# Splits of the second transform's matrices ahead of the data's own splits, and two output stores on another queue

## The chip, the cores and the metric

The kernel runs on one core of a Trainium2 chip. The metric is device time in microseconds (us) of one execution. An engine works through its own instructions in the order in which they were written, and waits only where a semaphore tells it to: TensorE (PE in the profile; PEld is its weight load), VectorE (DVE), ScalarE (ACT), GpSimd (POOL) and SyncE (SP). DMA transfers are issued by SP, ACT or POOL, each from its own queue in order.

## The reference, cut to what matters

The inputs are x (2048 x 640), two 2048 x 2048 matrices cr and ci, two 640 x 640 matrices wr and wi, and the two weights and biases of an MLP with 1536 hidden units, all in float32.

```python
xn = layernorm(x)
a = einsum("sd,ed->se", xn, wr); b = einsum("sd,ed->se", xn, wi)
y = einsum("ts,se->te", cr, a) - einsum("ts,se->te", ci, b)
out = x + y + gelu(xn @ w1 + b1) @ w2 + b2
```

## The kernel before, in words

Every product of two float32 matrices is made of three matmuls (`product`, L302 to L307): each operand is split into a high part in a reduced float32 format and a low part, the rest, and high times high, high times low and low times high are summed (L305, L306, L307). Low times low is left out. A split is a copy to the reduced format (`high`, on ACT, L191) followed by a subtraction (`low`, on DVE, L194). So before a matmul can run, somebody has split both of its operands.

The sequence transform is made first: xn stands still as weights (tiles `xab` and `xc`), and the columns of cr and ci move through the array. Its results, u from cr and v from ci, stay as sums in tiles `u1`, `u2`, `u` and `v1`, `v2`, `v`. The second transform then multiplies these sums by wr and wi. Both use a scheme that replaces eight products of blocks by seven, so each stage runs through seven products w = 0 to 6, and every product works on sums and differences of blocks, which are called forms here.

This case is about the second transform, the stage "y". It is run twice, each time for a pair of time tiles of 512 rows: a first pair (about 596 to 668 us in the profile) and the last pair (about 766 us to the end). In it the forms of wr and wi stand still as weights, five chunks of 128 columns for each product, and the sums u and v move. A product is done in steps u: step 0 uses chunks 0 and 1, step 1 the next two, step 2 the fifth. In the last pair step 3 adds two chunks of the MLP's second weight, whose hidden units were kept for this. "w4u1" below is step 1 of product 4. With three matmuls for each block, products 0, 1 and 2 have 18, 18 and 9 matmuls in steps 0 to 2 and products 3 to 5 have 12, 12 and 6; the last pair's step 3 has 18 or 12. Product 6 has 45 matmuls in the first pair. In the last pair it has 42 matmuls of 512 columns, and then 42 of 256 columns.

Three streams feed a step, and each has its own engines and buffers:

- The weights' forms. `load_g` (L1653, its DMA is L1672, on SP's queue) brings raw form number i = 5w + position into one of 7 places (first pair: `ws` x3, `gr_a` x2, `gr_b` x2) or 13 places (last pair: also six in `xab`). The load into a place is issued when the step that used it is written, and so it waits for that step's matmuls. `split_g(b, stop)` (L1677) then splits all forms below `stop`: the high part on ACT (L191), the low part on POOL (L1682), not on DVE.
- The moving forms. `form(n)` (L551) splits the sums for step n: high on ACT, low on DVE, into one of 3 slots of `as` (five slots in the last pair, two of them in `r`). The slot is free when the matmuls of the step before in it are through, so the form that is written in step n waits for step n's matmuls (first pair: it is for step n + 3; last pair: n + 5). ACT stands in that wait.
- The work beside (`hidden_beside`, L1685): additions on DVE that make the next sums, copies out of the matmuls' accumulators (`copy`, L1720, on ACT), transposes, and output stores (`store`, L1358).

At the end of each step the loop at L1941 writes: the work to be done ahead (`pre`), then the moving forms that are due, then the work beside (`post`), then `split_g`. That is the order on ACT. The stores of the last pair's outputs go to queues that are named in the call: `out_a` (L1731) for tile 1's columns, `out_b` (L1757) for tile 2's.

Of the kernel before, what the change touches and what calls it, by code (L numbers as in the profile page):

```python
# [17 lines left out]
B = 32  # L18
# [9 lines left out]
def kernel(  # L28
# [45 lines left out]
    nc = tc.nc  # L74
# [8 lines left out]
    ND = D // P  # L83
# [106 lines left out]
    def high(h, s):  # L190
        nc.scalar.activation(h, s, AF.Copy)  # L191
# [11 lines left out]
    def rows_of(ap, t):  # L203
        return ap[t * TB : (t + 1) * TB].rearrange("(n r) d -> r n d", r=B)
# [329 lines left out]
    def steps_in(st):  # L534
        return 2 if st[0] == "s" else ND // 2 + 1 if st is not stages[-1] else NLATE
# [164 lines left out]
    last = 1  # L700
# [653 lines left out]
    def store(t, src, c0, c1, *queues):  # L1354

        queues = queues or (nc.sync,)
        for q in range(Q):
            queues[q % len(queues)].dma_start(  # L1358
                rows_of(out, t)[:, :, q * DQ + c0 : q * DQ + c1], src[q * B : (q + 1) * B]
            )  # L1360
# [316 lines left out]
    def split_g(b, stop):  # L1677

        for i in range(split_to.get(b, 0), min(stop, NW * ND)):
            h, l = (GT[b, i][:, k] for k in range(2))  # L1680
            high(h, l.bitcast(F32))
            nc.gpsimd.tensor_tensor(l, l.bitcast(F32), h.bitcast(F32), op=ALU.subtract)  # L1682
        split_to[b] = max(stop, split_to.get(b, 0))

    def hidden_beside(b, n):  # L1685


        ta, tb = blocks[b - 1][1], blocks[b][1]
        last = b == len(blocks) - 1
        x_, y_, z_ = (banks[:, k : k + 2] for k in (X, Y, Z))  # L1690
        us, vs = bank(US), bank(VS)
        ya = yo[ta]

        def s(which, k):
            return sums[(ta, tb)[which], k]
# [14 lines left out]
        def columns(k):  # L1710

            return s(1 if last else 0, ("u1", "u2")[k]).rearrange("p a b -> p (a b)").rearrange("p (n e) -> p n e", n=NB)
# [16 lines left out]
            return f  # L1729

        def out_a(c0, c1):  # L1731
            return lambda: store(ta, ya[:, :, c0:c1], c0, c1, nc.gpsimd if c0 else nc.sync) if last else None

        def first_two():
            add(A["two"][:, 2:], A["two"][:, 2:], y_)
            to(ya[:, :, : 2 * B], A["two"][:, 2:], f"ya2_{ta}", out_a(0, 2 * B))()
# [18 lines left out]
            return f  # L1755

        def out_b(k):  # L1757
            return lambda: store(tb, columns(k), 2 * k * B, 2 * (k + 1) * B, *(((nc.gpsimd,), (nc.sync, nc.scalar))[k] if last else ()))

        def last_columns():  # L1760

# [166 lines left out]
    for kind, what in stages:  # L1928
        b = blocks.index(what) if kind == "s" else b
        count = NW * steps_in((kind, what)) if (kind, what) != stages[-1] else NW * NLATE  # L1930
        for n in range(first, first + count):
            w, u = entries[n][2:]
            if kind == "s":
                sequence_entry(n, what, w, u)
                pre, post = beside(*what, n - first)
            else:
                hidden_entry(n, b, w, u)
                pre, post = hidden_beside(b, n - first)
            for f in later:
                f()  # L1940
            later.clear()  # L1941
            for f in pre:
                f()
            while made <= n + 3 + min(max(n - LASTY + 2, 0), 2):
                form(made)
                made += 1
            for f in post:
                f()
            if kind == "y":
                done = w * ND + (min(2 * u + 2, ND) if u < 3 else ND)  # L1950
                split_g(b, done + (4 if u < 3 else ND))
        first += count
        if n + 1 < len(entries):
            X, Y, Z = Y, Z, X
        if kind == "y":
            put_off.clear()
# [45 lines left out]
```

## Time and profile before

| | us |
|---|---|
| median of the timed executions | 876.92 (lowest 876.74) |
| profiled execution | 871.97 |
| its span | 870.2 |
| PE busy | 848.1 (97%) |
| DVE busy | 703.8 (81%) |
| ACT busy | 387.6 (45%) |
| POOL busy | 162.8 (19%) |

In rows of the timeline the first number is the start in us from the span's start, the second the duration in us; then come engine, line, operation and tiles, and in brackets the idle time of that engine just before, with what ended it. A matmul's duration covers its way through the array, and the next one starts before it is over, so the pace of PE is read from start to start. In rows of the windows, each stretch has its length and then for PE, PEld, DVE, ACT and POOL the busy time and in brackets the number of instructions, followed by the granted clock, the DMA share and GB/s. Some matmul records can be missing.

### The profile page before, as it was taken

The page shows a single profiled execution, that of the slowest core. Times are in us where ns is not written, and L with a number is a line of the kernel's source. Part 1 is how long each engine was busy: PE and PEld are TensorE (multiplying, and loading weights), DVE is VectorE, ACT ScalarE, POOL GpSimd, SP SyncE. Part 2 cuts the span into 40 slices and gives each one's busy share as a digit, 9 for nine tenths or more (in the row PEclk, how much of TensorE's full clock was granted, in tenths as well). Part 3 has the DMA queues.
Part 4 walks back from the last instruction along what each step waited for, and adds up shares of the span by engine and source line. Part 5 has one row for each costly group of instructions (what it writes and reads, how often), then busy time and mean ns, then how long its engine had stood idle before and what let it go on. Part 6 is the DMA issues. An engine that isn't in the chain of part 4 may idle for free.

```text
span 870.2 us, 10835 instructions
## 1 busy us (share of the span) xinstructions
PE 848.1 (97%) x3719; PEld 695.6 (80%) x3719; DVE 703.8 (81%) x865; ACT 387.6 (45%) x566; POOL 162.8 (19%) x211
## 2 busy tenths in 40 slices
PE   8999999999999999999999999999989999999887
PEld 7888888888888888888888888887867888878665
DVE  6979886558478898898878799896988888768993
ACT  7655654444466634443433423233453232555450
POOL 3340021145000000000000000012753000334453
PEclk9999999999999999999999999999999999999999
DMA  7996576699689794965365985372226992261333
GB/s 228 283 253 167 125 193 203 188 282 294 222 241 419 180 207 114 230 156 159 85 182 162 293 198 134 96 186 63 79 77 182 268 268 72 82 254 43 86 87 73
DMA packets 197255, 154.69 MB, mean 178 GB/s; under 512 B 58000, under 2 KB 177808, under 8 KB 196688
## 3 DMA queue, kind: packets, MB, share of 16 engines
q1 hardware_dynamic: 185984, 122.73, 54.5%
q0 software_dynamic: 9040, 30.74, 10.5%
q10 hardware_dynamic: 2176, 0.52, 0.3%
q8 instruction: 29, 0.48, 0.2%
q14 instruction: 26, 0.21, 0.1%
HBM read 108.08 MB, written 41.94 MB: 172 GB/s over the span
## 4 chain that ended last, share of the span: by engine, by line
PE 83%; issue 6%; POOL 5%; DVE 3%; DMA 2%; SPq 1%; ACT 0%; POOLq 0%; DVEq 0%; ACTq 0%
PE banks L307 25%; PE banks L305 24%; PE banks L306 24%; PE banks L327 9%; POOL gr_b L1682 1%; POOL xab L1682 1%; POOL gr_a L1682 1%; POOL ws L1682 1%; DVE as L194 1%; SPq L1672 0%; DMA row<-in_A_x_dram 0%; DMA u<-ys 0%; DMA xab<-wsum 0%; DVE xab L453 0%; DMA ws<-wsum 0%
## 5 line engine op out<-in xcount | busy, mean ns | idle before, releaser
L191 ACT ACTIVATE as<-r 128x1024 fp32r<-128x1024 f32 x80 | 85.0, 1062 | 172.0 <-PE banks L307 148.0
L306 PE MATMUL banks<-as,xab 128*128 128x512 f32 (+1 forms) x375 | 145.5, 388 | 0.0
L307 PE MATMUL banks<-as,xab 128*128 128x512 f32 (+1 forms) x375 | 145.5, 388 | 0.0
L305 PE MATMUL banks<-as,xab 128*128 128x512 f32 (+1 forms) x375 | 145.4, 388 | 0.0
L194 DVE TENSOR_TENSOR as<-r,as 128x1024 fp32r<-128x1024 f32 x80 | 97.2, 1216 | 38.7 <-ACT as L191 38.6
L305 PE MATMUL banks<-as,xc 128*128 128x512 f32 x244 | 94.9, 389 | 0.0
L306 PE MATMUL banks<-as,xc 128*128 128x512 f32 x244 | 94.9, 389 | 0.0
L307 PE MATMUL banks<-as,xc 128*128 128x512 f32 x244 | 94.9, 389 | 0.0
L1682 POOL TENSOR_TENSOR ws<-ws 128x384 fp32r<-128x384 f32 (+1 forms) x24 | 31.6, 1328 | 321.4 <-DVE u L453 297.3
L306 PEld LDWEIGHTS banks<-as,xab 128*128 128x128 f32 x375 | 70.4, 188 | 14.5
L305 PEld LDWEIGHTS banks<-as,xab 128*128 128x128 f32 x375 | 70.4, 188 | 14.4
L307 PEld LDWEIGHTS banks<-as,xab 128*128 128x128 f32 x375 | 70.4, 188 | 14.4
L191 ACT ACTIVATE as<-rt 128x1024 fp32r<-128x1024 f32 x37 | 39.3, 1062 | 76.9 <-PE banks L307 61.2
L327 PE MATMUL banks<-xt,xab 128*128 128x512 f32 x240 | 56.6, 390 | 0.0
L194 DVE TENSOR_TENSOR as<-rt,as 128x1024 fp32r<-128x1024 f32 x37 | 45.5, 1230 | 12.2 <-ACT as L191 12.1
L306 PEld LDWEIGHTS banks<-as,xc 128*128 128x128 f32 x244 | 45.8, 188 | 9.5
L305 PEld LDWEIGHTS banks<-as,xc 128*128 128x128 f32 x244 | 45.8, 188 | 9.5
L307 PEld LDWEIGHTS banks<-as,xc 128*128 128x128 f32 x244 | 45.8, 188 | 9.5
L327 PEld LDWEIGHTS banks<-xt,xab 128*128 128x128 f32 x240 | 45.0, 188 | 9.3
L305 PE MATMUL banks<-hs,xc 128*128 128x512 f32 x120 | 46.7, 389 | 0.0
L306 PE MATMUL banks<-hs,xc 128*128 128x512 f32 x120 | 46.7, 389 | 0.0
L307 PE MATMUL banks<-hs,xc 128*128 128x512 f32 x120 | 46.7, 389 | 0.0
(316 smaller groups left out, 1790.7 us busy)
## 6 DMA issues: line engine op xcount, KB each, us to landing
raw<-in_A_dft_seq_re_dram SPq DMA_DIRECT2D x64, 256.0 KB, 5.3
raw<-in_A_dft_seq_im_dram SPq DMA_DIRECT2D x64, 256.0 KB, 5.0
w1r<-in_B_w_dram SPq DMA_DIRECT2D x144, 80.0 KB, 3.2
forms_ab<-xab SPq DMA_DIRECT2D x4, 1280.0 KB, 9.6
row<-xn SPq DMA_DIRECT2D x14, 320.0 KB, 6.0
w2r<-in_B_w_dram SPq DMA_DIRECT2D x12, 320.0 KB, 4.9
forms_c<-xc SPq DMA_DIRECT2D x4, 896.0 KB, 7.7
wturn<-row POOLq DMA_DIRECT2D x10, 320.0 KB, 4.2
```

What stands on the lines that cost most here:

```text
L191: nc.scalar.activation(h, s, AF.Copy)
L194: nc.vector.tensor_tensor(l, s, h.bitcast(F32), op=ALU.subtract)
L305: nc.tensor.matmul(acc, wh, mh, start=first, stop=False, skip_group_check=goes_on)
L306: nc.tensor.matmul(acc, wh, ml, start=False, stop=False, skip_group_check=goes_on)
L307: nc.tensor.matmul(acc, wl, mh, start=False, stop=last, skip_group_check=goes_on)
L327: nc.tensor.matmul(acc, W1[i][:, a, j * P : (j + 1) * P], XT[j][:, b], start=n == 0, stop=n == len(steps) - 1)
L1682: nc.gpsimd.tensor_tensor(l, l.bitcast(F32), h.bitcast(F32), op=ALU.subtract)
```

## The change

Two things change, in this stage alone.

First, `split_g` is called ahead of the loop that makes the moving forms, no longer behind the work beside. The numbers up to which it splits stay the same in each step, but for the first step of each pair: there it is 4 forms now, and was 6.

Second, two output stores of the last pair, four DMAs each, leave POOL's queue for SP's: that of tile 1's last 32 columns of each quarter (`out_a` with c0 > 0, called from `odd`) and that of tile 2's first 64 columns (`out_b(0)`). The store in `yb4` stays on POOL's.

```diff
         def out_a(c0, c1):
-            return lambda: store(ta, ya[:, :, c0:c1], c0, c1, nc.gpsimd if c0 else nc.sync) if last else None
+            return lambda: store(ta, ya[:, :, c0:c1], c0, c1) if last else None
...
         def out_b(k):
-            return lambda: store(tb, columns(k), 2 * k * B, 2 * (k + 1) * B, *(((nc.gpsimd,), (nc.sync, nc.scalar))[k] if last else ()))
+            return lambda: store(tb, columns(k), 2 * k * B, 2 * (k + 1) * B, *(((nc.sync,), (nc.sync, nc.scalar))[k] if last else ()))
...
             for f in pre:
                 f()
+            if kind == "y":
+                done = w * ND + min(2 * u + 2, ND)
+                split_g(b, done + (2 if done == 2 else 4 if u < 3 else ND))
             while made <= n + 3 + min(max(n - LASTY + 2, 0), 2):
                 form(made)
                 made += 1
             for f in post:
                 f()
-            if kind == "y":
-                done = w * ND + (min(2 * u + 2, ND) if u < 3 else ND)
-                split_g(b, done + (4 if u < 3 else ND))
```

The order of PE's and of DVE's instructions stays as it was. On ACT, in the first pair around w2u1 to w3u1, the rows of before are these. `as<-u` and `as<-v` are the high parts of moving forms (of w3u1, w3u2, w4u0 and w4u1 here), L1720 is the copy of an accumulator over the sum v1, and `gr_a`, `gr_b` and `ws` are high parts of wr's and wi's forms.

```order
L191 ACTIVATE as_2704<-u2_1_0_4406 128x1024 [waits DVE_49,PE_49,Activation_49]
L191 ACTIVATE ws_4042<-ws_4042 128x256 [waits DMAHW4_49,Pool_49]
L191 ACTIVATE gr_a5_4638<-gr_a5_4638 128x256 [waits DMAHW5_49,Pool_49]
L191 ACTIVATE as_2704<-u_1_0_4270 128x512 [waits DVE_49,PE_49,Activation_49]
L191 ACTIVATE gr_a5_4638<-gr_a5_4638 128x256 [waits DMAHW6_49,Pool_49]
L191 ACTIVATE as_2704<-v1_1_0_4542 128x1024 [waits PE_49,Activation_49]
L1720 ACTIVATE v1_1_0_4542<-banks_75 128x1024 [waits DVE_49]
L191 ACTIVATE gr_b5_4639<-gr_b5_4639 128x256 [waits DMAHW7_49,Pool_49]
L191 ACTIVATE gr_b5_4639<-gr_b5_4639 128x256 [waits DMAHW0_49,Pool_49]
L191 ACTIVATE as_2704<-v2_1_0_4360 128x1024 [waits PE_49]
```

The same place in the changed kernel:

```order
L191 ACTIVATE ws_4042<-ws_4042 128x256 [waits DMAHW4_49,Pool_49]
L191 ACTIVATE gr_a5_4638<-gr_a5_4638 128x256 [waits DMAHW5_49,Pool_49]
L191 ACTIVATE as_2704<-u2_1_0_4406 128x1024 [waits DVE_49,PE_49,Activation_49]
L191 ACTIVATE gr_a5_4638<-gr_a5_4638 128x256 [waits DMAHW6_49,Pool_49]
L191 ACTIVATE as_2704<-u_1_0_4270 128x512 [waits DVE_49,PE_49,Activation_49]
L191 ACTIVATE gr_b5_4639<-gr_b5_4639 128x256 [waits DMAHW7_49,Pool_49]
L191 ACTIVATE gr_b5_4639<-gr_b5_4639 128x256 [waits DMAHW0_49,Pool_49]
L191 ACTIVATE as_2704<-v1_1_0_4542 128x1024 [waits PE_49,Activation_49]
L1720 ACTIVATE v1_1_0_4542<-banks_75 128x1024 [waits DVE_49]
L191 ACTIVATE ws_4042<-ws_4042 128x256 [waits DMAHW1_49,Pool_49]
L191 ACTIVATE ws_4042<-ws_4042 128x256 [waits DMAHW2_49,Pool_49]
L191 ACTIVATE as_2704<-v2_1_0_4360 128x1024 [waits PE_49]
```

The two splits of `gr_b` have moved from behind the moving form of v1 and the copy L1720 to ahead of both; two splits of `ws`, which stood behind the moving form of v2, now stand between the copy and that form.

On POOL, in the last pair, the store of tile 1's last columns stood ahead of low parts of `gr_b` (first used in w3u0 and w3u1):

```order
 L1682 TENSOR_TENSOR ws_4042<-ws_4042 128x384 [waits DMAHW2_49,PE_49,Activation_49]
 L1682 TENSOR_TENSOR ws_4042<-ws_4042 128x256 [waits DMAHW3_49,PE_49,Activation_49]
-L1358 DMA out_0_dram<-yo1_5289 32x16x32 [waits DVE_49]
-L1358 DMA out_0_dram<-yo1_5289 32x16x32 [waits DMASW6_49]
-L1358 DMA out_0_dram<-yo1_5289 32x16x32 [waits DMASW7_49]
-L1358 DMA out_0_dram<-yo1_5289 32x16x32 [waits DMASW0_49]
 L1682 TENSOR_TENSOR gr_b7_5679<-gr_b7_5679 128x256 [waits DMAHW4_49,PE_49,Activation_49]
 L1682 TENSOR_TENSOR gr_b7_5679<-gr_b7_5679 128x256 [waits DMAHW5_49,PE_49,Activation_49]
```

The four DMAs are gone from there. The store of tile 2's first columns leaves POOL in the same way, from ahead of the last five low parts, which product 6 uses.

On SP, in the changed kernel, the first of the two stores stands between loads of wr's and wi's forms (`ws` for w5u0 and w5u1, and `gr_b` for w5u2):

```order
L1672 DMA ws_4042<-wsum_65 128x256 [waits DMAHW2_49,PE_49,Pool_49]
L1358 DMA out_0_dram<-yo1_5289 32x16x32 [waits DMAHW3_49,DVE_49]
L1358 DMA out_0_dram<-yo1_5289 32x16x32 [waits DMAHW4_49]
L1358 DMA out_0_dram<-yo1_5289 32x16x32 [waits DMAHW5_49]
L1358 DMA out_0_dram<-yo1_5289 32x16x32 [waits DMAHW6_49]
L1672 DMA ws_4042<-wsum_65 128x256 [waits DMAHW7_49,PE_49,Pool_49]
L1672 DMA ws_4042<-wsum_65 128x256 [waits DMAHW0_49,PE_49,Pool_49]
L1672 DMA gr_b7_5679<-wsum_65 128x256 [waits DMAHW1_49,PE_49,Pool_49]
```

Ahead of it there are no stores other than tile 1's first 64 columns of each quarter, as before; the four rows of `yo1` are new between the loads. The second store stands behind all loads of the stage, ahead of the stores of tile 2's middle columns.

## The prediction, made before the changed kernel was run

> **What bounds the kernel now.** I read the page's head first, then busy times by stage, and then the stage that the change touches, matmul by matmul.
>
> ```profile
> span 870.2 us, 10835 instructions
> 668.00:766.00 98.00, 98.00 (x434) 81.12 (x434) 82.29 (x75) 34.69 (x36) 9.97 (x12) 1.00 0.70 182
> 595.70:668.00 72.30, 66.06 (x271) 50.96 (x271) 59.98 (x49) 31.97 (x54) 43.31 (x32) 0.98 0.35 102
> 766.00:866.00 100.00, 90.43 (x400) 72.44 (x398) 83.06 (x94) 43.50 (x80) 44.36 (x45) 0.98 0.34 99
> 613.00:636.20 23.20, 20.68 (x92) 16.79 (x90) 23.04 (x19) 10.33 (x19) 13.60 (x10) 1.00 0.28 82
> 793.90:837.10 43.20, 36.58 (x161) 29.61 (x159) 42.91 (x44) 21.50 (x40) 21.56 (x22) 1.00 0.35 89
> ```
>
> TensorE bounds the kernel. Between the two pairs it runs without a gap: 434 matmuls in 98.00 us, 0.226 us each, which I take as 0.227 from neighbouring starts (655.27 and 655.51 below differ by 0.24, others by 0.22 or 0.23). In the pairs (rows 3 and 4) it has gaps. There lies all that this change can win: it touches no other stage. The last two rows matter as much. Over 23 us in the first pair and 43 us in the last one, VectorE (third busy time) has no gap worth the name.
>
> How much PE loses where: the first matmul of a product to that of a later one, less 0.227 us for each matmul between. First pair:
>
> ```profile
> 595.74 0.39 PE L305 MATMUL banks<-as,ws 128*128 128x512 f32 x1
> 607.68 0.39 PE L305 MATMUL banks<-as,gr_b 128*128 128x512 f32 x1
> 633.29 0.39 PE L307 MATMUL banks<-as,gr_a 128*128 128x512 f32 x1
> 636.49 0.50 PE L305 MATMUL banks<-as,gr_b 128*128 128x512 f32 x1 [2.81 <-ACT gr_b L191]
> 639.13 0.63 PE L305 MATMUL banks<-as,gr_b 128*128 128x512 f32 x1
> 639.56 0.63 PE L306 MATMUL banks<-as,gr_b 128*128 128x512 f32 x1
> 646.98 0.50 PE L307 MATMUL banks<-as,gr_a 128*128 128x512 f32 x1 [0.93 <-POOL gr_a L1682]
> 655.27 0.40 PE L307 MATMUL banks<-as,ws 128*128 128x512 f32 x1
> 655.51 0.39 PE L305 MATMUL banks<-as,gr 128*128 128x512 f32 x1
> 668.06 0.39 PE L305 MATMUL banks<-as,xab 128*128 128x512 f32 x1
> ```
>
> Product 0 takes 11.94 us for 45 matmuls (10.2): lost 1.7. Products 1 to 5 take 47.83 us for 180 (40.9): lost 7.0. Product 6 takes 12.55 us for 45: lost 2.3. Together 11.0 us. The stalls named here end with ACT or POOL splitting a weight form, the thing that the change moves. After the longest, at w3u2, matmuls start 0.43 us apart (639.13, 639.56): a part of the 7.0 is a halved pace.
>
> Last pair:
>
> ```profile
> 765.98 0.39 PE L305 MATMUL banks<-r,ws 128*128 128x512 f32 x1
> 782.41 0.39 PE L305 MATMUL banks<-as,gr_a 128*128 128x512 f32 x1
> 810.97 0.39 PE L305 MATMUL banks<-as,ws 128*128 128x512 f32 x1
> 816.44 0.50 PE L307 MATMUL banks<-as,gr_b 128*128 128x512 f32 x1 [3.50 <-POOL gr_b L1682]
> 837.28 0.47 PE L305 MATMUL banks<-r,xab 128*128 128x512 f32 x1 [3.30 <-DVE v L453]
> 848.51 0.39 PE L305 MATMUL banks<-as,gr_b 128*128 128x512 f32 x1
> 865.86 0.28 PE L307 MATMUL banks<-as,xab 128*128 128x256 f32 x1
> ```
>
> Product 0: 16.43 us for 63 matmuls (14.3), lost 2.1. Products 1 and 2: 28.56 for 126 (28.6), nothing. Products 3 and 4: 26.31 for 84 (19.1), lost 7.2, which is the two gaps of 3.50 and 3.30 with their restarts. Product 5: 11.23 for 42 (9.5), lost 1.7. Product 6, from 848.51 to about 866.0: 17.5 for 42 long matmuls and 42 of half length (14.6), lost 2.9. Together 13.9 us. The two pairs lose 24.9 us: no result of this change can be far below 871.97 − 24.9.
>
> **First pair, part by part.** No work is added or removed: each split costs the same and leaves its engine earlier. In product 0 the first `gr_a` split waits behind v1's form, which waits for w0u0; its load is older than the stage. It now stands ahead of that form, so its 1.7 us go. In product 6 the fourth form's split waits behind a moving form that waits for w5u2, the step just ahead of it; now it waits only for the form of w5u1. Its 2.3 us go too.
>
> The middle is not so simple. These are ACT and DVE there:
>
> ```profile
> 635.11 1.02 ACT L1720 ACTIVATE v<-banks 128x1024 f32<-128x1024 f32 x1 [2.99 <-DVE as L194]
> 636.03 0.71 ACT L191 ACTIVATE gr_b<-gr_b 128x256 fp32r<-128x256 f32 x2
> 636.64 1.05 ACT L191 ACTIVATE as<-v 128x1024 fp32r<-128x1024 f32 x1
> 633.86 1.21 DVE L194 TENSOR_TENSOR as<-v,as 128x1024 fp32r<-128x1024 f32 x1
> 637.72 1.30 DVE L194 TENSOR_TENSOR as<-v,as 128x1024 fp32r<-128x1024 f32 x1 [1.51 <-ACT as L191]
> 643.98 1.23 DVE L194 TENSOR_TENSOR as<-u,as 128x1024 fp32r<-128x1024 f32 x1 [1.00 <-ACT as L191]
> 646.71 1.30 DVE L194 TENSOR_TENSOR as<-u,as 128x1024 fp32r<-128x1024 f32 x1 [0.37 <-ACT as L191]
> 652.63 1.18 DVE L194 TENSOR_TENSOR as<-v,as 128x1024 fp32r<-128x1024 f32 x1
> ```
>
> The `gr_b` splits at 636.03 stand behind the copy at 635.11, and PE waits for them. Ahead of both, they run near 629, and PE would go on at 633.5. But the copy writes over v1, so it waits for the low part that ends at 635.07, and that one comes at the end of the gapless stretch of DVE. v2's form stands behind the copy as before: ACT 636.64, low part until 639.02, no earlier than now. PE would want it at 633.5 + 1.36 (w3u2) + 2.72 (w4u0) = 637.6. So a shorter wait for the moving form takes the place of the wait for the weight. From there to the form of w6u0 (low part until 653.81) DVE idles only 1.00 and 0.37 us, waiting for ACT and behind it for PE. If PE is early these go, and that low part ends at 652.4. w6u0 can start 0.2 us ahead of it, at 652.2 in place of 655.5: of 7.0 us, 3.3 are won and 3.7 remain. The 1.7 us of product 0 shift all this as a whole, since the stretch of DVE begins with a form that waits for PE. First pair: 1.7 + 3.3 + 2.3 = 7.3 us; bounds 1.7 and 11.0.
>
> **Last pair.**
>
> ```profile
> 813.02 2.62 POOL L1358 DMA_DIRECT2D out_dram<-yo  x4 [8.81 <-DVE yo L453]
> 815.65 1.42 POOL L1682 TENSOR_TENSOR gr_b<-gr_b 128x256 fp32r<-128x256 f32 x2
> 835.92 1.21 DVE L453 TENSOR_TENSOR v<-banks,xc 128x1024 f32<-128x1024 f32 x1
> 845.62 2.57 POOL L1358 DMA_DIRECT2D out_dram<-u  x4 [9.05 <-DVE u L453]
> ```
>
> Product 0 again waits for one split behind a form: 2.1 us go. The gap of 3.50 at 816.44 is the first store's: POOL stood 8.81 us for DVE's addition and took 2.62 to issue, with the low part of `gr_b` behind it. Without the store there, that low part is ready well ahead. But the next gap ends with DVE's addition at 835.92, which must read the accumulator before product 5 writes it, and it is an instruction of the gapless stretch from 793.9 to 837.1. PE arrives 3.8 us earlier and waits 3.8 us longer. That stretch begins with a form that waits for PE, so only the 2.1 us come through. I keep the 1.7 of product 5 too: matmuls there start up to 0.43 us apart, as after 636.49, and the gap ahead of them grows.
>
> In product 6, POOL's last five low parts stand behind the second store (9.05 + 2.57 us). Without it they follow their ACT halves, from about 836 on for the first; product 6 starts near 846. The 2.9 us go: DVE's last forms end at 848.3 and shift with the 2.1. Last pair: 2.1 + 2.9 = 5.0 us; bounds 2.1 and 13.9.
>
> The Trainium skill (DMA: Bandwidth & Descriptors, "Issuing engines are not separate DMA queues") says that another issuing engine saves only its issue time, usually small. By it the second store would be worth at most its 2.57 us, an estimate of 860.0 for the sum below; the rows show a standing queue of 9.05 us ahead of the issue.
>
> On SP, behind the first store stand the loads of `ws` and `gr_b` for w5u1 and later. The store waits for an addition that ends at 812.7, so they leave near 815 instead of 812; w5u1 comes after 837. That cover is 20 us: cost nothing. If DVE slipped far enough, product 6's 2.9 us would be lost again.
>
> Sum: 871.97 − 7.3 − 5.0 = **859.7** in the profiled execution. The median shown, 876.92, lies 4.95 above it; with the same offset **864.6**.
>
> **The rivals.**
>
> ```profile
> gr_b<-wsum SPq DMA_DIRECT2D x4, 128.0 KB, 2.0
> u<-ys SPq DMA_DIRECT2D x2, 512.0 KB, 4.4
> 815.51 3.51 DVE L453 TENSOR_TENSOR u<-u,u 128x512 f32<-128x512 f32 x1
> 632.12 0.68 DVE L194 TENSOR_TENSOR as<-u,as 128x512 fp32r<-128x512 f32 x1
> ```
>
> *Loads hold ACT.* A split at the head of ACT waits for its load, with moving forms behind it. From the freeing of a place to the form's use lie 30 matmuls (6.8 us) in products 3 to 6; needed are the landing (2.0 for 128 KB), split 0.4, high part 1.05, low part 1.2, together 4.7. That leaves 2.1 us, little with DVE full. If it fails, the middle and the end of the first pair win nothing: 1.7 + 5.0 = 6.7, time 870.2.
>
> *Slower.* The same wait, with landings of 10 us (the slowest above is 4.4; the point is 4.1): in the first pair forms are late by 5.9 us in each of products 3 to 6, and by 2.5 in products 0 to 2, where 45 matmuls (10.2 us) lie between; together 31. They replace the 9.3 us that products 1 to 6 lose now, and the other 6.7 are still won: +15, time 892. Against it: the DMA share in the pairs is about 0.35.
>
> *POOL beside DVE.* An addition of 512 columns takes 3.51 us beside POOL's low parts (815.51, 815.65) and 0.68 alone. Two more low parts of about 1.25 us fall into DVE's gapless stretch if splits leave a step earlier: +2.5, time 867.1. The Trainium skill (SBUF — State Buffer, "Who interferes with whom") says that a DVE instruction with two SBUF inputs and a GpSimd one that reads SBUF exclude each other for a whole instruction. By it these two would cost their full length, as I set; the stretch shows less on average, 21.56 us of POOL inside 42.91 us of DVE.
>
> *All gaps go*, if DVE's instructions shrink once POOL's are elsewhere: 876.92 − 24.9 = 852.0. Against it: 99% busy in both stretches.
>
> *The store holds SP*: 2.9 us less, 867.5. *Nothing comes through*, each wait turning into DVE's: 876.9.
>
> **How the numbers follow.** Forecast 864.6: 0.45. Loads hold ACT 0.25, POOL beside DVE 0.10, store on SP 0.06, all gaps go 0.07, nothing 0.04, slower 0.03. From 857.5 (the first pair's 11.0 in full, the last pair's 5.0 and half of its 7.2) to 873.5 (half of what the load rival leaves) lie all but the last three. Two per cent, about what a measurement of this kernel can tell from no change, are 17.5 us: faster than 859.4 takes the rival of all gaps and a little of the forecast, 0.08; slower than 894.5 takes a part of its rival, 0.02; within, 0.90.
>
> **What would show it.** First pair: no ACT-ended stall near w3u2, a stall near w4u1 to w6u0 that ends with `as` L194 on DVE, and 64 to 66 us for the stage. Last pair: no gap in product 3, a gap of about 7 us ahead of product 5 that ends with DVE's addition, product 6 without POOL's stalls. ACT idle that ends with loads ahead of `gr` or `ws` splits, with moving forms late behind it, would prove the first rival. If DVE shows idle time inside its stretches while PE waits, my bound is wrong.

## The result, and the profile after

| | before | after |
|---|---|---|
| median of the timed executions (4 each) | 876.83 us | 864.43 us |
| lowest | 873.04 us | 863.99 us |
| profiled execution | 871.97 us | 865.42 us |
| its span | 870.2 us | 863.6 us |

One execution of before, of 3667 us, is left out of the comparison. The ratio of the mean times of the others is 0.9874, with a 95% interval of [0.9842, 0.9907]: 1.3% faster, within the 2% that count as no change. The forecast was 864.6 us, so the median is met within 0.2 us. The way to it is met only in part: the two profiled executions lie 6.55 us apart, where the sum said 12.3.

These are the head of the page and the windows of the changed kernel: the first pair, the last pair, and DVE's stretch in the last pair.

```profile
span 863.6 us, 10830 instructions
597.20:665.20 68.00, 62.90 (x271) 50.12 (x271) 61.35 (x49) 31.69 (x53) 46.14 (x32) 1.00 0.36 106
763.20:859.20 96.00, 89.21 (x400) 73.72 (x398) 83.66 (x94) 42.76 (x80) 46.79 (x37) 0.95 0.36 102
788.70:831.90 43.20, 36.43 (x150) 29.58 (x149) 38.97 (x48) 18.73 (x36) 22.82 (x16) 0.88 0.37 90
```

The first pair takes 68.0 us, 72.3 before; the last pair takes 95.8 (763.21 to 859.05 below), 99.9 before. Together that is 8.3 us, more than the 6.55 between the two profiled executions: in the changed kernel's the first pair starts 1.5 us later (597.25 against 595.74) and the end behind the last matmul is 0.2 longer, outside what the change touches. In the last row DVE is busy for 38.97 of 43.20 us. The prediction called that stretch gapless and built a bound on it.

PE's boundaries of products and its waits in the first pair, from the timeline of the changed kernel:

```profile
597.25 0.39 PE L305 MATMUL banks<-as,ws 128*128 128x512 f32 x1
607.45 0.39 PE L305 MATMUL banks<-as,gr_b 128*128 128x512 f32 x1
636.89 0.50 PE L305 MATMUL banks<-as,gr_b 128*128 128x512 f32 x1 [1.90 <-ACT v L1720]
645.45 0.50 PE L306 MATMUL banks<-as,gr_a 128*128 128x512 f32 x1 [1.22 <-DVE as L194]
648.80 0.50 PE L306 MATMUL banks<-as,gr_b 128*128 128x512 f32 x1 [0.34 <-DVE as L194]
652.83 0.39 PE L305 MATMUL banks<-as,gr 128*128 128x512 f32 x1
654.57 0.50 PE L306 MATMUL banks<-as,gr 128*128 128x512 f32 x1 [1.35 <-DVE as L194]
656.53 0.50 PE L306 MATMUL banks<-as,ws 128*128 128x512 f32 x1 [0.29 <-DVE as L194]
665.29 0.39 PE L305 MATMUL banks<-as,xab 128*128 128x512 f32 x1
```

Every wait for a weight's split is gone. In its place stand one wait for a copy and four for the low part of a moving form. Product 0 takes 10.20 us, which is 45 times 0.227: nothing lost. Products 1 to 5 lose 45.38 − 40.9 = 4.5 us (7.0 before). Product 6 takes 12.46 us and loses 2.3, as before, with DVE where POOL was.

The last pair:

```profile
763.21 0.39 PE L305 MATMUL banks<-r,ws 128*128 128x512 f32 x1
806.05 0.39 PE L305 MATMUL banks<-as,ws 128*128 128x512 f32 x1
817.16 0.39 PE L306 MATMUL banks<-r,xab 128*128 128x512 f32 x1
824.31 0.79 PE L307 MATMUL banks<-r,xab 128*128 128x512 f32 x1 [6.77 <-POOL xab L1682]
824.90 0.63 PE L305 MATMUL banks<-r,xab 128*128 128x512 f32 x1
825.33 0.63 PE L306 MATMUL banks<-r,xab 128*128 128x512 f32 x1
834.78 0.39 PE L305 MATMUL banks<-r,xab 128*128 128x512 f32 x1
844.30 0.39 PE L305 MATMUL banks<-as,gr_b 128*128 128x512 f32 x1
859.05 0.28 PE L307 MATMUL banks<-as,xab 128*128 128x256 f32 x1
```

Products 0 to 2 take 42.84 us for 189 matmuls (42.9) and lose nothing. Products 3 and 4 take 28.73 us for 84 (19.1) and lose 9.7, 2.5 more than before. All of it is one gap of 6.77 us at w4u0, with half the pace behind it: from 824.90 twelve matmuls in a row start 0.43 us apart, and the granted clock of the stretch is 0.88 (last row of the windows above), 1.00 in the prediction's row of before. Product 5 loses nothing (9.52 us). Product 6 takes 14.75 us up to the start of its last matmul, for which 14.45 are needed, and loses 0.3 (2.9 before).

The gap's cause stands on POOL and DVE, in the same timeline. The last of these rows comes from the group of POOL's low parts of `xab` between 815 and 828 us; its three numbers are the shortest, the median and the longest duration in ns.

```profile
815.91 8.35 POOL L1682 TENSOR_TENSOR xab<-xab 128x256 fp32r<-128x256 f32 x1 [7.42 <-ACT xab L191]
816.04 0.75 DVE L194 TENSOR_TENSOR xc<-xab,xc 128x256 fp32r<-128x256 f32 x2
816.72 1.22 DVE L453 TENSOR_TENSOR v<-v,u 128x1024 f32<-128x1024 f32 x1
...
822.46 1.22 DVE L453 TENSOR_TENSOR rt<-rt 128x1024 f32<-128x1024 f32 x1
827.51 1.23 DVE L194 TENSOR_TENSOR r<-u,r 128x1024 fp32r<-128x1024 f32 x1 [3.83 <-ACT r L191]
L1682 POOL TENSOR_TENSOR xab<-xab x5: 721/724/8351, 815.9 to 826.3; 128x256 fp32r<-128x256 f32 x5
```

One low part, of a kind that takes 0.72 us at the median, took 8.35. Beside it DVE ran a row of additions and low parts without a break until 823.68, all with both inputs in SBUF, at their full speed (1.22 us each). 0.58 us behind the end of that row the low part was through. Then the loop closed the other way: DVE stood 3.83 us for a high part on ACT, which stood behind PE, which had stood for POOL.

### The profile page after: what moved, and what is told of

Its sections match the earlier page's. It is cut to its first block, busy times and chain, and to the rows that moved or that the text cites. A ratio compares the mean times of both kernels' runs of the same rounds, so it can differ in the third digit from the quotient of the medians.

```text
span 863.6 us, 10830 instructions
## 1 busy us (share of the span) xinstructions
PE 844.3 (98%) x3719; PEld 696.6 (81%) x3719; DVE 705.6 (82%) x865; ACT 387.3 (45%) x566; POOL 168.2 (19%) x203
## 4 chain that ended last, share of the span: by engine, by line
PE 86%; DVE 6%; issue 4%; POOL 2%; ACT 1%; DMA 1%; SPq 0%; POOLq 0%; ACTq 0%; DVEq 0%
PE banks L306 25%; PE banks L307 25%; PE banks L305 25%; PE banks L327 9%; DVE as L194 2%; POOL xab L1682 2%; DVE u L453 1%; PE banks L680 1%; DVE v L453 1%; ACT as L191 0%; DVE xo L453 0%; POOL ws L1682 0%; DMA gr_b<-wturn 0%; DVE rt L453 0%; DVE rt L514 0%
```

## The experiments

The first four kernels ran beside before on one chip, the next four on another, then two and two. Before's median was 875.55, 874.44, 875.09 and 876.01 us there, so kernels of different groups are compared by their ratio to it. The ratios are those of mean times.

| kernel | median us | ratio to before | interval |
|---|---|---|---|
| splits moved, stores not | 865.86 | 0.9885 | [0.9851, 0.9919] |
| stores moved, splits not | 879.28 | 1.0043 | [1.0020, 1.0066] |
| splits two forms further ahead | 862.57 | 0.9851 | [0.9815, 0.9887] |
| one transpose added | 861.50 | 0.9837 | [0.9803, 0.9871] |
| first pair: two pieces later | 864.21 | 0.9882 | [0.9856, 0.9907] |
| the same, and `odd` as the break | 861.76 | 0.9855 | [0.9826, 0.9884] |
| the same, and the added transpose | 860.98 | 0.9850 | [0.9821, 0.9879] |
| stores alone, with the transpose | 875.20 | 1.0004 | [0.9984, 1.0025] |
| first pair thinned further | 861.03 | 0.9833 | [0.9802, 0.9864] |
| stores alone, transpose, ACT free | 870.82 | 0.9952 | [0.9930, 0.9974] |
| two low parts on DVE | 863.53 | 0.9860 | [0.9834, 0.9885] |
| before, a second trace | 876.14 | one execution | |

**The two halves of the change.** One kernel keeps the new place of the splits and puts both stores back on POOL's queue:

```diff
-            return lambda: store(ta, ya[:, :, c0:c1], c0, c1) if last else None
+            return lambda: store(ta, ya[:, :, c0:c1], c0, c1, nc.gpsimd if c0 else nc.sync) if last else None
...
-            return lambda: store(tb, columns(k), 2 * k * B, 2 * (k + 1) * B, *(((nc.sync,), (nc.sync, nc.scalar))[k] if last else ()))
+            return lambda: store(tb, columns(k), 2 * k * B, 2 * (k + 1) * B, *(((nc.gpsimd,), (nc.sync, nc.scalar))[k] if last else ()))
```

> The moved splits alone: both output stores stay on POOL's queue as before. If the two parts add up as in the prediction's sum, the first pair wins what it won in the changed kernel (4.3 us, 72.3 to 68.0) and the last pair only the 2.1 us of product 0: 6.4 us faster than before, with POOL's stalls of product 6 (2.9 us) still there and a gap of about 3.5 us in product 3 ended by POOL's gr_b. If the stores did the work in the last pair, the same. If the new long gap of product 4 (6.8 us, ended by POOL's xab) comes from the moved splits, it is here too; if it comes from the moved stores, product 4 has none here.

The other is before with these two lines of the change alone:

> The moved stores alone: the splits stand where they stood before. By the prediction's sum the last pair wins the 2.9 us of product 6, and the 3.5 us of product 3 come back later in front of product 5: 2.9 us faster than before, first pair as before (72.3 us). The rival, that POOL's freedom is worth all of its 8.8 us in front of product 3, gives about 6 us faster. If the long gap of product 4 ended by POOL's xab comes from the stores, it shows here.

The splits alone give 865.86 us, 1.4 more than the whole change; the two kernels' timed executions overlap (864.08 to 867.50 here, 863.99 to 865.42 there). That is 9.7 us faster than before on that chip, where 6.4 had been expected. The stores alone were expected to be 2.9 us faster; they are slower than before by 0.43%, and the interval excludes no change. The change's gain is the splits' doing. The long gap at w4u0 goes with the stores: the trace of the stores alone has it, that of the splits alone has not.

In the kernel with the splits alone POOL's low parts of `xab` ran as in before (five in 5.42 us). PE's waits in its last pair:

```profile
811.52 0.50 PE L307 MATMUL banks<-as,gr_a 128*128 128x512 f32 x1 [1.75 <-POOL gr_a L1682]
824.82 0.50 PE L306 MATMUL banks<-as,xc 128*128 128x512 f32 x1 [0.99 <-DVE as L194]
831.66 0.47 PE L305 MATMUL banks<-r,xab 128*128 128x512 f32 x1 [4.06 <-DVE v L453]
847.05 0.50 PE L307 MATMUL banks<-r,xab 128*128 128x512 f32 x1 [0.45 <-POOL xab L1682]
```

The first is the first store's, which still stood on POOL's queue ahead of low parts. The third is the one that the prediction had expected ahead of product 5. The fourth is in product 6, which lost 1.1 us (842.91 to 858.44), with the second store on POOL's queue, too.

In the kernel with the stores alone two gaps hurt. These are PE, POOL, and ACT at the second one:

```profile
827.33 0.79 PE L307 MATMUL banks<-r,xab 128*128 128x512 f32 x1 [7.70 <-POOL xab L1682]
855.41 0.80 PE L305 MATMUL banks<-r,xab 128*128 128x512 f32 x1 [5.10 <-ACT xab L191]
818.92 8.35 POOL L1682 TENSOR_TENSOR xab<-xab 128x256 fp32r<-128x256 f32 x1 [6.61 <-ACT xab L191]
853.82 0.89 ACTq L1785 DMA_DIRECT2D out_dram<-u  x2
854.84 0.52 ACT L191 ACTIVATE xab<-xab 128x384 fp32r<-128x384 f32 x1 [8.45 <-issue]
```

The first is the 8.35 us low part again, in the old order of splits. The second speaks against the prediction's reading of product 6: POOL's queue was free of the store, and the time was lost all the same, since the last split's high part stood on ACT behind two output DMAs of `late_rows` (L1785), which were issued when DVE's addition was over (at 853.79).

**What makes the low part long.** Two explanations were open: the split that feeds it is late (its high part stands behind the copy L1720), or POOL is locked out by DVE's row. The first kernel brings all splits of the last pair two forms further ahead:

```diff
-                split_g(b, done + (2 if done == 2 else 4 if u < 3 else ND))
+                split_g(b, done + (2 if done == 2 else ND if u == 3 else 6 if b == len(blocks) - 1 else 4))
```

> The changed kernel, with the last pair's forms split two further ahead in each step. Theory one (the prediction's: VectorE's work sets when product 5 may start): nothing changes, 0 to 1 us. Theory two (in the changed kernel one low part on POOL for w4u0 starts late, behind the copy at 813.9, and then stands 8.35 us because VectorE's additions of two SBUF operands follow each other without a break): the low parts of w4u0 are made before that stretch, the 6.8 us gap and the halved pace behind it (2.6 us) go, and VectorE's own idle 3.8 us go with them: 5 to 8 us faster than the changed kernel.

The median fell to 862.57 us, but the gap stayed, at 5.65 us, with another low part that began at 815.06 and took 9.49. The 5 to 8 us that the second theory had given didn't come. With the splits earlier a low part, now a later one, meets the row all the same, and is held for as long. Of the 1.9 us won, 1.1 are the shorter gap.

The second adds work. Behind the transform's addition in step 3.0 of the last pair, DVE transposes an accumulator that nobody needs any more:

```diff
             post += [steps[n]] if n in steps else []
+            if n == 12:
+                post.append(lambda: turned(us, f"gap_{tb}"))
```

> The changed kernel with one instruction more: VectorE transposes a 128x512 block out of an accumulator that nobody needs any more into a scratch tile (0.7 us), behind the first addition of w3u0 (at 817.9 in the changed kernel's profile). Work is only added. Theory one (VectorE's work bounds this stretch): 0 to 1 us slower. Theory two (POOL is locked out by back-to-back additions): an instruction with its input in PSUM leaves a break in which POOL's waiting low part of 0.7 us gets in, so the 6.8 us gap of product 4 shrinks to 1 or 2 us, and the kernel is 3 to 6 us FASTER though it does more.

The time was 861.50 us, 2.9 less than the changed kernel's. DVE, POOL and PE in its trace:

```profile
816.05 0.71 DVE L1377 STREAM_TRANSPOSE gap<-banks 128x512 f32<-128x512 f32 x1
814.11 8.34 POOL L1682 TENSOR_TENSOR xab<-xab 128x256 fp32r<-128x256 f32 x5 [7.41 <-DMA gr_b<-wturn]
816.78 0.50 PE L307 MATMUL banks<-r,xab 128*128 128x512 f32 x1 [1.03 <-POOL xab L1682]
828.16 0.47 PE L305 MATMUL banks<-r,xab 128*128 128x512 f32 x1 [2.84 <-DVE v L453]
```

The transpose reads one input, out of an accumulator. During it the first of POOL's five low parts came through (2.61 us, ended at 816.72). Behind it the two engines took turns: several of DVE's instructions took 1.75 to 1.77 us in place of 1.22, and no further low part more than 1.8. The gap at w4u0 shrank to 1.03. Ahead of product 5 there now is the wait for DVE's addition that the prediction had expected, 2.84 us.

The third makes two of POOL's low parts on DVE, the 8.35 us one among them:

```diff
-            nc.gpsimd.tensor_tensor(l, l.bitcast(F32), h.bitcast(F32), op=ALU.subtract)
+            eng = nc.vector if b == len(blocks) - 1 and i in (21, 22) else nc.gpsimd
+            eng.tensor_tensor(l, l.bitcast(F32), h.bitcast(F32), op=ALU.subtract)
```

> The changed kernel with two of POOL's low parts, those of the `xab` forms number 21 and 22 (for w4u0 and w4u1 of the last pair; the first of them took 8.35 us in the changed kernel), made by DVE: two instructions more in DVE's row, 0.4 us each by their half share of a 128x512 one, and two less on POOL. Nothing is left out. Theory 2 (POOL's low part was locked out by DVE's row): no 6 to 7 us gap at w4u0 that ends with POOL; in its place PE waits about 3 us for DVE's addition v L453 ahead of product 5, as with the added transpose; last pair 92.5 to 94 us, time 861 to 863. Rival (the gap is DVE's or ACT's lateness whatever POOL does, since that split's high part stood behind the copy L1720 until 815.42): a gap of 5 us or more stays at w4u0, now ended by DVE's L194, time 864 to 866.

863.53 us lies between what the two expected. The lock-out's expectation missed what its own mechanism says, that the next low part of POOL meets the same row:

```profile
815.70 9.02 POOL L1683 TENSOR_TENSOR xab<-xab 128x256 fp32r<-128x256 f32 x1 [8.54 <-ACT xab L191]
822.92 1.22 DVE L194 TENSOR_TENSOR r<-u,r 128x1024 fp32r<-128x1024 f32 x1
824.77 0.79 PE L307 MATMUL banks<-as,xab 128*128 128x512 f32 x1 [4.79 <-POOL xab L1683]
```

It took 9.02 us and ended at 824.72, again 0.58 behind the last of DVE's instructions that read SBUF twice (822.92 + 1.22). That the late split makes this gap is excluded: the two low parts that had been late did not wait for POOL here, and the gap followed the row.

The fourth puts the added transpose into the kernel with the stores alone:

> The kernel with the stores on SP alone (old place of the splits; 879.28 us, a gap of 7.70 us at 827.33 that ends with POOL's low part of `xab`), with the added transpose at step 3.0 of the last pair. Theory 2 (the gap is a POOL low part locked out by DVE's row of additions, which the store on POOL's queue kept apart in the kernel before by making POOL late): the gap goes or shrinks below 2 us, POOL's five low parts there take 5 to 7 us in place of 11.10, and the time falls by 4 to 7 us, to 872 to 875. Rival (the gap is the moved store's doing on SP, through the loads behind it): the gap stays at 6 to 8 us, time 878 to 881.

The ratio fell from 1.0043 to 1.0004, about 3.4 us, though the intervals still touch; the gap at w4u0 fell from 7.70 to 1.96. The time is just above the 872 to 875 expected, and POOL's low parts there were not as quick as they should have been (six in 10.01 us). The second gap stayed (5.82 us at 852.68). So the lock-out was most of what made the stores alone slower than before. The wait behind ACT's DMAs was still there. The fifth kernel takes that one away too, by issuing these DMAs on SP:

```diff
-                    (nc.sync, nc.scalar)[q % 2].dma_start(
+                    nc.sync.dma_start(
```

> The kernel with the stores on SP alone and the added transpose (875.20 us), with the four DMAs of the store `late_rows` all on SP's queue, where two of them stood on ACT's. In product 6 ACT stood 9.17 us until these two were issued at 851.09, with the split of the last `xab` form behind them, and PE lost 5.82 us there. Nothing is left out. Theory 3 (not the store on POOL's queue but the place of the splits behind the work beside, ACT's DMAs among it, makes product 6 lose time): the 5.82 us and the half pace behind it go, 868 to 871. Rival (PE waits there for the same addition on DVE in another way, for instance for a moving form): 873 to 876.

The ratio is 0.9952, another 0.5% less. PE in its trace:

```profile
835.25 0.77 PE L305 MATMUL banks<-r,xab 128*128 128x512 f32 x1 [4.56 <-DVE v L453]
847.49 0.39 PE L305 MATMUL banks<-as,gr_b 128*128 128x512 f32 x1
862.15 0.28 PE L307 MATMUL banks<-as,xab 128*128 128x256 f32 x1
```

Product 6, from the second row to the third, takes 14.66 us where its matmuls need 14.45. PE waits for DVE's addition ahead of product 5 instead. The time and the trace are as theory 3 had them, with one correction: the splits stand at their old place here and product 6 loses nothing, so what costs is not the place itself but an output DMA that waits at the head of a queue with splits behind it, on ACT or on POOL. Moving the splits ahead and moving the DMAs away are two remedies for the same thing. How much of the 2.9 or 7.2 us of before (second trace below) was the store on POOL's queue was not measured by itself. This trace differs from the last one in the lock-out, too: here POOL and DVE took turns from the start, so a part of the 0.5% can be that.

**What is left in the first pair.** Two pieces of DVE's work are written later:

```diff
-            6: [to(ya[:, :, : 2 * B], y_, f"ya2_{ta}"), t2(2)],
-            7: [odd],
+            6: [t2(2)],
...
-            18: [yb2],
-            19: [f6s[0]],
+            18: [yb2, to(ya[:, :, : 2 * B], y_, f"ya2_{ta}")],
+            19: [f6s[0], odd],
```

> The changed kernel, but in the first pair two pieces of the work beside, the transposed addition `ya2` (step 6) and `odd` (step 7), are written at steps 18 and 19. Nothing is left out; DVE has 5 instructions less in its stretch from step 6 to step 17. Theory 1 (DVE's full stretch, not ACT, sets what is left in products 3 to 6 of the first pair: the copy L1720 that PE waits for 1.90 us at 636.89 waits for a low part that DVE makes late, and four further stalls of 1.22, 0.34, 1.35 and 0.29 us end with DVE's `as` L194): these stalls go for the most part, with the half pace behind them; the first pair takes 62.5 to 65 us in place of 68.04, and the time is 859.5 to 862. Rival (ACT, held by the loads of `ws` 2.31 and `gr` 2.07 us, makes the forms late and DVE only follows): the stalls stay, 67 to 68.5 us, 863.5 to 865.5.

864.21 us, no gain, and a ratio of 0.9882: theory 1 missed its number. The trace tells why:

```profile
642.62 0.50 PE L306 MATMUL banks<-as,gr_a 128*128 128x512 f32 x1 [0.98 <-DVE as L194]
651.84 0.50 PE L306 MATMUL banks<-as,gr 128*128 128x512 f32 x1 [1.44 <-DVE as L194]
666.96 0.50 PE L305 MATMUL banks<-as,xab 128*128 128x512 f32 x1 [1.09 <-DVE yo L1377]
```

The wait for the copy (1.90) is gone, as theory 1 had it: with DVE free earlier, the low part that the copy waits for is early. The four waits for DVE's low parts stay, since DVE's work between the copy and them is as long as it was, and the late pieces make a new one of 1.09 at the pair's end. From one pair's start to the next it takes 165.36 us, 165.96 in the changed kernel.

With this and a break in the last pair, `odd` moved there in one kernel (it begins with a transpose out of an accumulator) and the added transpose in the other, the two gains were expected to add.

> As the kernel before this one (`ya2` and `odd` of the first pair late), and in the last pair `odd` stands behind the transpose of step 3.0, no longer at step 2.1. Nothing is left out or added. Theory 2 (POOL's low part of `xab` is kept from running through the whole row of DVE's additions that follow one another from 816.0 to 823.7; a transpose out of the accumulator in that row lets it in): `odd` begins with such a transpose, so the low part runs there and the gap of 6.77 us at w4u0 is gone; DVE then bounds the last pair and PE waits about 3 us for the addition v L453 ahead of product 5; last pair 92 to 94 us in place of 95.8, time 856 to 859 if theory 1 holds too. Rival (the transpose added in the earlier experiment helped by shifting DVE's work by 0.7 us, no more): `odd`'s two additions with it lengthen the row, the gap stays at 5 to 8 us or grows, last pair 95.5 to 98 us.

> The changed kernel with `ya2` and `odd` of the first pair late, and with the added transpose of the dead accumulator at step 3.0 of the last pair (0.7 us of DVE work whose result nobody reads). If the two causes are apart, each in its own pair, the gains add: 3 us of the last pair and the gain of the kernel with the late pieces alone, 856 to 859. If theory 1 fails, 861 to 862.

861.76 and 860.98 us. In the first PE has no wait for POOL at w4u0, against the rival; in the second one of 1.03 us is left. That `odd` serves as the break isn't shown: in its trace DVE's instructions are slowed, taking 1.84 and 1.75 us, from 813.34 on, so POOL was already through when `odd`'s transpose began at 816.79. Its additions make later forms late (1.67 us at 823.86), and the two kernels come out alike. Neither reached 856 to 859, for the first pair gave nothing; without that gain 861 to 862 had been expected.

The last kernel of this line also takes the transpose of `yb1` out of the stretch (step 14 to 16) and puts `ya2` and `odd` at step 17:

> As the changed kernel with the late pieces and the added transpose, but the first pair's stretch of DVE from 635 to 657 us is thinned further: the transposed part of `yb1` leaves step 14 for step 16, and `ya2` and `odd` stand at step 17 behind `yb1`'s second part, not at steps 18 and 19. Nothing is left out. Theory 1 in its second form (what is left in the first pair is DVE's own length between the form behind the copy, near 634.5, and the forms of product 6; each us taken out of it comes through): the stall of 1.56 us at 650.90 goes (the transpose ahead of that form takes 1.25), and the two stalls of 0.16 and 1.06 at the pair's end, which the late pieces made, go; the stalls near 641.60 and 644.96 stay, since the work ahead of them is the same. Gain 2 to 3.5 us, time 857.5 to 859. Rival (ACT, waiting for the loads of `ws` and `gr` for 2.06 and 2.17 us, makes those forms late): the stall at 650.90 stays at 1.2 us or more, and only the end's is won, 859.5 to 860.5.

861.03 us, no less than the one before, and outside what either theory had given. In its trace the wait that was 1.56 us at 650.90 is gone, as theory 1's second form had it, and a new one of 1.19 stands at 663.19 where the moved pieces are; from start to start the pair takes 164.21 us against 165.41. So DVE's length does set these waits; the places tried for the work, in the stretch and behind it, gave the timed executions no gain. ACT's waits for loads (2.06 and 2.17 us in the trace with two pieces later) stayed throughout and made nothing of DVE's late: from 635.61 on it has no idle time before 657.88.

Three kernels with the added transpose (861.50, 860.98 and 861.03 us) have lower medians than the changed kernel; their intervals don't tell them apart, and they overlap that of the changed kernel. The cleanest comparison is that of the kernel with the two later pieces without the transpose and with it, on one chip: 864.21 and 860.98 us, with five of six executions below the lowest of the other (863.49).

**A second trace of before.** Its timed executions lie between 870 and 882 us, those of the changed kernel within 1.5 us.

> The kernel before once more, for a second trace of it: its runs lie between 870 and 882 us, those of the changed kernel between 864.0 and 865.4. If POOL's low parts beside DVE's rows come out differently from run to run, this trace shows gaps in the last pair of other length or at other places than 3.50 at 816.44 and 3.30 at 837.28; the first pair's, which end with waits in a fixed order, stay within 0.5 us. If the spread comes from elsewhere (the granted clock, the start of the pairs), both pairs lose the same as before and start later.

This execution took 876.14 us, 4.17 more than the one that the prediction was worked out from. PE's boundaries in it, and its longest waits behind product 5:

```profile
596.10 0.39 PE L305 MATMUL banks<-as,ws 128*128 128x512 f32 x1
766.34 0.39 PE L305 MATMUL banks<-r,ws 128*128 128x512 f32 x1
838.74 0.47 PE L305 MATMUL banks<-r,xab 128*128 128x512 f32 x1 [1.20 <-ACT as L191]
848.36 0.39 PE L305 MATMUL banks<-as,gr_b 128*128 128x512 f32 x1
851.28 0.50 PE L307 MATMUL banks<-as,gr_b 128*128 128x512 f32 x1 [2.30 <-POOL gr_b L1682]
856.30 0.49 PE L305 MATMUL banks<-r,xab 128*128 128x512 f32 x1 [1.63 <-ACT xab L191]
870.04 0.28 PE L307 MATMUL banks<-as,xab 128*128 128x256 f32 x1
```

From the first pair's start to the last pair's it takes 170.24 us, to the hundredth what the first trace shows (595.74 to 765.98). Of the 4.17 us, 3.8 are in the last pair: 103.7 us against 99.9; the rest lies ahead of the first pair. Product 6 alone, from 848.36 to the last matmul at 870.04, takes 21.68 us and loses 7.2, where the first trace has 2.9. Those 4.3 us are nearly as much as the 4.95 that the prediction added as an offset. The wait of 2.30 follows the store on POOL's queue (issued from 847.63 on), that of 1.63 the two DMAs on ACT's. More than the waits differs: this execution's mean granted clock was 0.992, 0.996 in the first trace. Of the 17 executions of before beside the first four kernels, the five with 0.996 to 0.998 took 871.61 to 873.48 us and the five with 0.990 took 876.55 to 882.33, so the spread goes with the granted clock.

## Why the prediction was right, and where it was not

*The time* is right by luck, by two errors of one size. The sum was 12.3 us for the profiled execution, and the profiles differ by 6.55: 4.0 us short in the two pairs, and 1.7 lost outside them. The offset of 4.95 us was carried over unchanged, as if it lay outside the change's reach; after's median lies 0.99 below its profiled time. By two traces, before's offset was in large part product 6 of the last pair, which the first showed at 2.9 and the second at 7.2; in the changed kernel's one trace it is 0.3, and its executions lie within 1.5 us. That the whole spread sat there isn't shown: the kernel with ACT free lost nothing in product 6, and its executions spread over 6 us. One trace had been taken for the kernel. The lower end of the range has a slip: by its own terms it is 857.3, not 857.5.

*First pair: product 0* gave 1.7, as forecast. *Its middle* was forecast to keep 3.7 of 7.0 and keeps 4.5, with waits for DVE's low parts between w4u1 and w6u0 as said. But no ACT-ended wait was to be near w3u2, and one of 1.90 is there. The step that failed: "a shorter wait for the moving form takes the place of the wait for the weight". PE waits for the copy itself, because the matmuls of w4u0 write the accumulator that the copy reads; the prediction followed the copy on ACT and not to PE. *Product 6's 2.3* did not go. The step "now it waits only for the form of w5u1" is right for the weight's split; what was not asked is whether DVE's low parts would be there. They come 1.35 and 0.29 us late. Together 4.3 us were won in place of 7.3.

*Last pair: product 0's 2.1* came. *Products 3 and 4* were to keep 7.2, as a gap of about 7 us ahead of product 5 that ends with DVE's addition, and keep 9.7, as a gap at w4u0 that ends with POOL. The size is near, the cause is another. The step that failed: the bound from "the gapless stretch from 793.9 to 837.1", which held for the order of before and not when POOL's low part met DVE's row. The prediction named its own refutation, idle time of DVE inside the stretch while PE waits, and so it came: 3.83 us at 827.51. The bound itself was sound for DVE: as soon as the lock-out was broken, the wait for L453 was there (2.84, 2.98, 4.56 us), but for the stores alone with the transpose, where one of 1.53 us ends with ACT. *Product 5's 1.7* were to stay and are gone, with the clock's half pace now in product 4. *Product 6* came out as forecast by size, but its working gave all of it to the store on POOL, and the kernel with the stores alone loses 8.2 us there in its trace (2.9 and 7.2 in those of before), with ACT's DMAs ahead of the last split. Together 4.0 us in place of 5.0.

*The rivals.* "Loads hold ACT" did not come: ACT stood 2.31 and 2.07 us for loads of `ws` and `gr` in the first pair, but DVE has no idle time from 638.43 to 660.63, so no low part of DVE's was late for that. "POOL beside DVE" was the rival nearest to what came: it priced two more low parts at their own length, 2.5 us. The mechanism is that one, the price was not: 6.77 us and a halved pace. The row it was priced by had shown more: DVE's addition of 3.51 us began at 815.51 and ended at 819.02, 0.56 us behind the last of four low parts that POOL ran one after another (815.65 to 818.46). It had been held for the whole row, and not for one low part. The rival came in the first pair, too: DVE's same 49 instructions take 61.35 us there, 59.98 before. The Trainium skill (SBUF — State Buffer, "Who interferes with whom") states that a DVE instruction with two SBUF inputs contends with a GpSimd one that reads SBUF, that the contention is an exclusive lock which blocks the other fully for a whole instruction, and that a DVE instruction with at most one SBUF input, outside the two-port modes, does not contend. The traces agree, and show more: the blocked one can stay so through a whole row of instructions, about 7.7 us here, not only one. On the stores, the prediction weighed the Trainium skill (DMA: Bandwidth & Descriptors, "Issuing engines are not separate DMA queues"), by which another issuing engine saves little, and set it aside for the standing queue of 9.05 us. The kernel with the stores alone, 0.43% slower, shows no gain either, but it is no test of that sentence: what it lost went to the lock-out and to ACT's DMAs.

## What to carry to other kernels

An instruction that waits at the head of a queue holds all that stands behind it, so move what is ready ahead of what waits, and ask of every engine in turn what then comes last; here moving splits gave the gain, and moving stores little or none. Where a short instruction of GpSimd runs beside a busy VectorE that reads two operands from SBUF, look at its longest duration and not its mean, and place an instruction of VectorE that reads an accumulator where the other must come through. And take a second trace of a kernel whose times spread more than the effect to be forecast: the spread can sit in the very stage that the change touches.

## What the runs showed that was not expected

- A 128x256 subtraction on POOL took 8.35, 9.49, 9.02, 8.35 and 8.35 us (the changed kernel, further ahead, two low parts on DVE, stores alone, two pieces later), where 0.72 is the median in the changed kernel. Each ended 0.57 to 0.59 us behind the last of DVE's instructions in its row that read SBUF twice.
- Adding a transpose of 0.71 us to DVE, the fullest engine beside PE, made kernels faster: by 2.9 us in the medians of the changed kernel, by 3.2 where both ran on one chip.
- In before and with the splits alone, low parts at the same place went through beside DVE, with DVE slowed instead (1.75 or 1.76 us for an addition in place of 1.22). So it was in all three traces with the first store on POOL's queue, where POOL had stood idle 3.75 us ahead of them. Of the eleven with the store on SP's (idle 6.01 to 8.54 us), nine began locked out, four of these until the added transpose. Two did not, the kernel with `odd` moved and the one with ACT free, and the latter had the same order there and the same 6.61 us of idle time as the stores alone with the transpose, which was locked out. Where it came ahead of the row's pair of `xc` low parts, POOL's first low part started 0.13 or 0.14 us ahead of it in both outcomes. What decides is open, and one trace of a kernel doesn't say how often it happens.
- TensorE's pace halves behind some gaps and not behind others. After 6.77 us twelve matmuls ran at 0.43 us each (2.4 us lost beyond the gap). In the second trace of before, such stretches of 5 to 8 matmuls followed gaps at 636.85, 773.15, 818.43 and 856.30; in the first trace only those at 636.49 and 837.28. The Trainium skill (TensorE: Matmul & The Clock Gate, "What's actually happening") states a half clock after an idle window of about 3.4 us, counted by a free-running monitor, whose phase varies from run to run. That the same gap of 3.50 us ahead of product 3's `gr_b` was followed by half pace in one trace and not in the other agrees with it; that half pace also followed the gaps of 2.81 us at 636.49 and 1.22 us at 773.15, shorter than that window, is not what it states.
